# Conversion of W_out through PSUM, and weight sums in halves in other places, in an attention and feed-forward kernel

## The chip, the cores and the metric

The kernel runs on one core of a Trainium2 chip. The metric is the device time of one execution in microseconds (us), measured without a profiler. The profiled execution is a separate one; its span counts from the first to the last instruction.

The core has engines with an instruction stream each: TensorE (PE in the profile, its weight loads are PEld), VectorE (DVE), ScalarE (ACT), GpSimd (POOL), and SyncE (SP), which here only issues transfers (DMA). SBUF is the on-chip memory of 128 partitions, PSUM the smaller one that PE writes its products to; VectorE and ScalarE read and write both.

## The reference

Attention in which a query sees only keys of the same hash bucket, then two matrix products with a gated activation between them. Cut to what matters:

```
def _attn_ref(q, k, v, proj):            # q, k, v: 4 x 8 x 768 x 64, proj: 64 x 6
    q_bits, k_bits = (q @ proj > 0), (k @ proj > 0)
    mask = bucket(q_bits)[..., :, None] == bucket(k_bits)[..., None, :]
    scores = where(mask, q @ k.T / sqrt(64), -1e9)
    return softmax(scores) @ v

def _moe_ref(x, w_in, w_out):            # x: 3072 x 512, w_in: 512 x 2048, w_out: 2048 x 512
    h = x @ w_in
    g = h * (1.0 / (1.0 + np.exp(-1.702 * h)))
    return (g @ w_out).astype(np.float32)
```

The weights w_in and w_out come as numbers of 64 bits; the kernel reads them as pairs of 32-bit words (lo, hi) and makes float32 of them on the chip. This is called conversion below.

## The kernel before

The kernel has three stages. In *attention* PE makes scores and values, ScalarE the exponentials; VectorE converts W_in on the side, one chunk of 128 x 512 numbers at a time. In the *hidden layer* PE makes x @ w_in by one level of Strassen's method (seven products of quarters instead of eight): 24 steps of seven products of 128 x 512, three times 1024 tokens (sb) by eight blocks of 128 rows (mt). Each step stores seven blocks to memory (g_dram): the four activated results and three sums that the next stage needs. In the *output stage* PE makes g @ w_out by two levels of Strassen: 3 x 7 outer products (OUTER), each of seven inner products.

Strassen's method needs sums of the quarters of each factor (`sums_a` for weights, `sums_b` for the data):

```
    def sums_a(eng, a11, a12, a21, a22, s1, s2, s4):
        return [lambda: eng.tensor_tensor(s1, a21, a22, op=Alu.add),
                lambda: eng.tensor_tensor(a21, a11, a21, op=Alu.subtract),     # in place
                lambda: eng.tensor_tensor(s2, s1, a11, op=Alu.subtract),
                lambda: eng.tensor_tensor(s4, a12, s2, op=Alu.subtract)]
```

The conversion of one chunk, seven VectorE instructions and one of ScalarE (the `yield`s are places where other work goes between):

```
    def convert(cv, dst, src, queue=None):
        raw = cv.tile([P, CW, 2], U32, tag="raw", name="raw")
        (queue or loader[0]).dma_start(out=raw, in_=src)
        ...
        lo, hi = raw[:, :, 0], raw[:, :, 1]
        sign, bits, size = ...                                  # three tiles of 128 x 512 in SBUF
        yield
        nc.vector.scalar_tensor_tensor(sign, hi, 0x80000000, masks[0x40000000], op0=Alu.bitwise_and, op1=Alu.bitwise_or)
        nc.vector.scalar_tensor_tensor(bits, hi, 3, masks[0x7FFFFFFF], op0=Alu.logical_shift_left, op1=Alu.bitwise_and)
        yield
        nc.vector.tensor_tensor(bits, bits, sign, op=Alu.bitwise_xor)
        yield
        nc.vector.tensor_tensor(sign, bits, masks[0xFF800000], op=Alu.bitwise_and)
        nc.scalar.activation(size, hi.bitcast(F32), Act.Square)
        yield
        nc.vector.scalar_tensor_tensor(dst, of(lo), 2.0**-52, of(sign.bitcast(F32)), op0=Alu.mult, op1=Alu.mult)
        yield
        nc.vector.tensor_tensor(dst, of(bits.bitcast(F32)), dst, op=Alu.add)
        yield
        nc.vector.scalar_tensor_tensor(dst, of(size), (1.125 * 2.0**-15) ** 2, dst, op0=Alu.is_ge, op1=Alu.mult)
```

`masks[...]` is a column of 128 values spread over 512 elements, so it is a second operand in SBUF. `raw` has one buffer.

One step of the hidden layer:

```
            def hidden(sb, mt, mid=(), end=()):
                ...
                nc.scalar.copy(u, product(1))
                nc.vector.tensor_tensor(v, product(6), u, op=Alu.add)          # evictions: PSUM + SBUF -> SBUF
                nc.vector.tensor_tensor(c21, product(7), v, op=Alu.add)
                p = product(5)
                nc.vector.tensor_tensor(c22, p, c21, op=Alu.add)
                emit(c22, 3)                                                   # activation, store
                nc.vector.tensor_tensor(c12, p, v, op=Alu.add)
                nc.vector.tensor_tensor(u, product(2), u, op=Alu.add)
                emit(u, 0)
                for x in mid:
                    x()
                nc.vector.tensor_tensor(c12, product(3), c12, op=Alu.add)
                emit(c12)
                nc.vector.tensor_tensor(c21, product(4), c21, op=Alu.add)
                emit(c21, 2)
                for f, kept in zip(sums_b(nc.gpsimd, u, c12, c21, c22, v, t2, t4), ((4, v), (1, c12), (5, t2), (6, t4))):
                    f()                                                        # GpSimd's sums of g, stored
                    keep(*kept)
                for x in end:
                    x()
```

What is hung into the steps, and the places of the weights' sums (`rooms`: three sums for each of the seven outer products):

```
            rooms = [xT[:, 3, 0:W2]] + [w_room[:, i * W2 : (i + 1) * W2] for i in range(5)] + [s_room[:, 0:W2]]   # w_room: W_in's tile
            ...
                    if n == 1:
                        ...                                     # w_out_sb; wqs: its quarters and their sums
                        for i in (list(range(1, LATE + 1)) if late else []) + free[:FC]:
                            todo[i] = [lambda: next(steps)] * 2                # one conversion in step i
                        w_steps = sums_a(nc.vector, *wqs)
                        todo[3 * MT - 3], todo[3 * MT - 2] = w_steps[:2], w_steps[2:] + sums_a(nc.gpsimd, *w_quarters(OUTER[0]))
                    if n == 2:
                        ...                                     # two more PSUM banks for products: 6 -> 8
                    if n == 3 * MT - 3:
                        ...
                        fetch(0)
                    if sb == 0 and mt + 1 < MT:
                        for f in in_sums(mt + 1):               # GpSimd: sums of W_in for the next step
                            f()
                    x = sums_b(nc.vector, *quarters_x(sb + 1)) if mt == MT - 1 and sb + 1 < n1 else []
                    hidden(sb, mt, x[:3], x[3:] + todo.pop(n, []) + (g_sums(0) if n == 3 * MT - 1 else []))
            ...
            for n, (sb, o) in enumerate(steps_out):             # output stage
                if n + 1 < len(steps_out):
                    fetch(n + 1)
                if n + 1 < len(OUTER):
                    for f in sums_a(nc.gpsimd, *w_quarters(OUTER[n + 1])):     # inner sums of the next outer product
                        f()
                later_sums = g_sums(n + 1)                      # VectorE: sums of g for the next step
                ...
                ms[o] = product_of_halves(n, None if acc is None else ms[acc], after)
```

In `product_of_halves` the products come in the order 1, 2, 3, 6, 7, 5, 4; only from product 6 on are the sums of g (t2, t1, t4) needed. MT is 8, FC is 16, P is 128.

Of the kernel before, what the change touches and what calls it, by code (L numbers as in the profile page):

```python
# [8 lines left out]
F32 = mybir.dt.float32  # L9
BF16 = mybir.dt.bfloat16  # L10
I32 = mybir.dt.int32
U32 = mybir.dt.uint32
Act = mybir.ActivationFunctionType
Alu = mybir.AluOpType
AX = mybir.AxisListType
PSUM = bass.MemoryType.PSUM
# [3 lines left out]
P = 128  # L20
# [18 lines left out]
def kernel(  # L39
# [17 lines left out]
    nc = tc.nc  # L57
# [8 lines left out]
    KC, FC = DM // P, FF // P  # L66
# [70 lines left out]
    xT = const.tile([P, KC, N], F32, name="xT")  # L137
    w_in_sb = const.tile([P, KC, FF], F32, name="w_in_sb")
    s_in = const.tile([P, 3, KC // 2, FF // 2], F32, name="s_in")
# [9 lines left out]
    CW = 512  # L149


    masks = {}
    for x in (0x40000000, 0x7FFFFFFF, 0xFF800000):
        m = const.tile([P, 1], U32, name=f"mask_{x:x}")
        later.append((m, x))
        masks[x] = m.to_broadcast([P, CW])

    def convert(cv, dst, src, queue=None):

        raw = cv.tile([P, CW, 2], U32, tag="raw", name="raw")  # L160
        (queue or loader[0]).dma_start(out=raw, in_=src)

        def of(x):
            return x if len(dst.shape) == 2 else x.rearrange("p (x r) -> p x r", r=dst.shape[2])

        lo, hi = raw[:, :, 0], raw[:, :, 1]
        sign = cv.tile([P, CW], U32, tag="sign", name="sign")
        bits = cv.tile([P, CW], U32, tag="bits", name="bits")
        size = cv.tile([P, CW], F32, tag="size", name="size")
        yield  # L170

        nc.vector.scalar_tensor_tensor(sign, hi, 0x80000000, masks[0x40000000], op0=Alu.bitwise_and, op1=Alu.bitwise_or)  # L172
        nc.vector.scalar_tensor_tensor(bits, hi, 3, masks[0x7FFFFFFF], op0=Alu.logical_shift_left, op1=Alu.bitwise_and)  # L173
        yield
        nc.vector.tensor_tensor(bits, bits, sign, op=Alu.bitwise_xor)  # L175
        yield

        nc.vector.tensor_tensor(sign, bits, masks[0xFF800000], op=Alu.bitwise_and)  # L178

        nc.scalar.activation(size, hi.bitcast(F32), Act.Square)  # L180
        yield
        nc.vector.scalar_tensor_tensor(dst, of(lo), 2.0**-52, of(sign.bitcast(F32)), op0=Alu.mult, op1=Alu.mult)  # L182
        yield
        nc.vector.tensor_tensor(dst, of(bits.bitcast(F32)), dst, op=Alu.add)  # L184
        yield

        nc.vector.scalar_tensor_tensor(dst, of(size), (1.125 * 2.0**-15) ** 2, dst, op0=Alu.is_ge, op1=Alu.mult)

    wi = w_in.bitcast(U32).rearrange("(kc ki) (f two) -> kc ki f two", ki=P, two=2)
    wo = w_out.bitcast(U32).rearrange("(fc fi) (d two) -> fc fi d two", fi=P, two=2)  # L190
# [3 lines left out]

    LATE = 2

    def sums_a(eng, a11, a12, a21, a22, s1, s2, s4):

        return [lambda: eng.tensor_tensor(s1, a21, a22, op=Alu.add),
                lambda: eng.tensor_tensor(a21, a11, a21, op=Alu.subtract),  # L200
                lambda: eng.tensor_tensor(s2, s1, a11, op=Alu.subtract),
                lambda: eng.tensor_tensor(s4, a12, s2, op=Alu.subtract)]

# [8 lines left out]
    K2, F2 = KC // 2, FF // 2  # L212
# [448 lines left out]
    def feed_forward(tag, late=()):  # L661
# [3 lines left out]
        F4, TH = FC // 4, XT // 2  # L665
        n1 = N // (2 * XT)

        LEFT = dict(zip(range(1, 8), (0, 1, 6, 3, 4, 5, 2)))
        RIGHT = dict(zip(range(1, 8), (0, 2, 3, 6, 4, 5, 1)))
        OUTER = (1, 6, 7, 5, 2, 3, 4)  # L670
        with ExitStack() as fctx:
            stage_ctx = fctx.enter_context(ExitStack())
            stage = stage_ctx.enter_context(tc.tile_pool(name=f"stage{tag}", bufs=2, side="right"))
            late = list(late)
            sets = [fctx.enter_context(tc.tile_pool(name=f"f0{tag}", bufs=6, space=PSUM, side="right"))]
            todo, turn = {}, [-1]
# [46 lines left out]

            wqs = []

            w_room, s_room = (x.rearrange("p k f -> p (k f)") for x in (w_in_sb, s_in[:, 2]))
            W2 = 3 * F4 * P
            rooms = [xT[:, 3, 0:W2]] + [w_room[:, i * W2 : (i + 1) * W2] for i in range(5)] + [s_room[:, 0:W2]]
            wholes = [xT[:, i, 4 * XT : 6 * XT] for i in range(4)] + [t_x[:, i].rearrange("p k t -> p (k t)") for i in range(2)]
            wholes = [x.rearrange("p (q t) -> p q t", q=4) for x in wholes]  # L730

            def w_quarters(o):

                w = wqs[LEFT[o]]
                x = [w[:, i, F4 * j : F4 * (j + 1), :] for i in range(2) for j in range(2)]
                s = rooms[OUTER.index(o)].rearrange("p (i c d) -> p i c d", i=3, c=F4)
                return x + [s[:, i] for i in range(3)]

            steps_out = [(sb, o) for sb in range(n1) for o in OUTER]
            raw_g = [None, s_in[:, 0:2].rearrange("p i k f -> p (i k f)").rearrange("p (c t) -> p c t", t=XT)]  # L740

            def fetch(n):
                sb, o = steps_out[n]
                for h in range(2):
                    cs = slice(h * F4, (h + 1) * F4)
                    loader[0].dma_start(out=raw_g[n % 2][:, cs], in_=g_dram[len(LEFT) * sb + RIGHT[o], :, cs, :])
# [14 lines left out]
            def g_sums(n):  # L761
                return sums_b(nc.vector, *g_quarters(n)) if n < len(steps_out) else [lambda: None] * 4
# [54 lines left out]
                after(3)  # L817
                return m

            def conversions(cv, chunks):  # L820

                gens = [convert(cv, *x) for x in chunks]
                next(gens[0])
                for i, x in enumerate(gens):
                    for y in gens[i + 1 : i + 2]:
                        next(y)
                    for at, _ in enumerate(x):
                        if at == 1:
                            yield
                    yield  # L830

            MT = FC // 2
            for sb in range(n1):
                for mt in range(MT):
                    n = sb * MT + mt
                    if n == 1:
                        wop = fctx.enter_context(tc.tile_pool(name=f"wo{tag}", bufs=1))
                        cv_ctx = fctx.enter_context(ExitStack())
                        cv = cv_ctx.enter_context(tc.tile_pool(name=f"cv{tag}", bufs=1))


                        w_out_sb = wop.tile([P, 4, FC, P], F32, name="w_out_sb")
                        wqs += [w_out_sb[:, 2 * i : 2 * i + 2, MT * k : MT * (k + 1), :] for i in range(2) for k in range(2)]
                        wqs += [xT[:, i, 0 : 4 * XT].rearrange("p (h c d) -> p h c d", h=2, d=P) for i in range(3)]
                        places = [w_out_sb[:, :, fc, :].rearrange("p r x -> p x r") for fc in range(FC)]
                        steps = conversions(cv, late + [(places[fc], wo[fc]) for fc in range(FC)])
                        free = [i for i in range(LATE + 1, 3 * MT) if i % MT != MT - 1]
                        for i in (list(range(1, LATE + 1)) if late else []) + free[:FC]:
                            todo[i] = [lambda: next(steps)] * 2
                        w_steps = sums_a(nc.vector, *wqs)  # L850
                        todo[3 * MT - 3], todo[3 * MT - 2] = w_steps[:2], w_steps[2:] + sums_a(nc.gpsimd, *w_quarters(OUTER[0]))
                    if n == 2:
                        sets.append(fctx.enter_context(tc.tile_pool(name=f"f1{tag}", bufs=2, space=PSUM)))
                        turn[0] = 7
                    if n == 3 * MT - 3:
                        cv_ctx.close()
                        gp = fctx.enter_context(tc.tile_pool(name=f"gp{tag}", bufs=1))
                        raw_g[0] = gp.tile([P, FC // 2, XT], F32, name="raw_g")
                        fetch(0)
                    if sb == 0 and mt + 1 < MT:  # L860
                        for f in in_sums(mt + 1):
                            f()
                    x = sums_b(nc.vector, *quarters_x(sb + 1)) if mt == MT - 1 and sb + 1 < n1 else []
                    hidden(sb, mt, x[:3], x[3:] + todo.pop(n, []) + (g_sums(0) if n == 3 * MT - 1 else []))
                    yield
            stage_ctx.close()
            st2 = fctx.enter_context(tc.tile_pool(name=f"st2{tag}", bufs=1, side="right"))
# [1 line left out]
            ms, pending = {}, []  # L869
            for n, (sb, o) in enumerate(steps_out):  # L870
                final = n + 1 == len(steps_out)
                if n + 1 < len(steps_out):
                    fetch(n + 1)
                if n + 1 < len(OUTER):
                    for f in sums_a(nc.gpsimd, *w_quarters(OUTER[n + 1])):
                        f()
                later_sums = g_sums(n + 1)
                m = wholes[n % len(wholes)]

# [13 lines left out]
                        written(sb, 0, (0,), loader + [nc.scalar])  # L893

                acc = {6: 1, 7: 6, 2: 1, 3: 6, 4: 7}.get(o)
                ms[o] = product_of_halves(n, None if acc is None else ms[acc], after)

                def flat(x):
# [65 lines left out]
```

## Time and profile before

| | before |
|---|---|
| time, median of 3 | 954.63 us (953.36 to 955.95) |
| span of the profiled execution | 951.8 us |
| mean granted PE clock | 0.975 |
| PE, DVE busy | 890.9, 805.4 us |
| ACT, POOL busy | 312.4, 348.5 us |

Busy shares are means over stages with different limits, so the profile is read by stages: in the row of slices each digit is the busy share, in tenths, of one fortieth of the span. In a timeline line stand the start, the duration, the engine, the line of the kernel, the operation with output<-inputs, their shapes, the count, and in brackets the idle time before it and what ended it. In the list of waits stand engine, line, what was waited for, and then the total in us, how often, and the longest. The ends of matmuls in the profile are modelled; their starts are what the text uses.

### The profile page before, as it was taken

To read this page: it belongs to the slowest core of one execution; us is meant where nothing else is said; L and a number is where in the kernel's file an instruction comes from. 1 tells how busy PE (TensorE), PEld (TensorE's weight loads), DVE (VectorE), ACT (ScalarE), POOL (GpSimd) and SP (SyncE) were. 2 spreads that over 40 slices of the span, in tenths; PEclk is the share of its full clock that TensorE was granted. 3 is DMA by queue.
4 is the path that set the end of the run, shared out by engine and by line. 5 is a ranking of instruction groups with operands and counts; after the bars stand their busy time and mean duration, and the time that the engine had idled before them with its cause. 6 is when DMAs were issued, how large, how long until landed. Compare 5 with 4: busy or idle time off the path is not lost.

```text
span 951.8 us, 11992 instructions
## 1 busy us (share of the span) xinstructions
PE 890.9 (94%) x4077; PEld 509.6 (54%) x4077; DVE 805.4 (85%) x1048; ACT 312.4 (33%) x519; POOL 348.5 (37%) x274
## 2 busy tenths in 40 slices
PE   9999999999999999985998859989788999999995
PEld 4444444444444444432443324433577888888884
DVE  4798888888899648999799997999797986887795
ACT  5667666576675422212122122122100000000000
POOL 4233323333224536683453434546995000000000
PEclk9999999999999999998999979999999999999998
DMA  4543454443541024443444434446735566557634
GB/s 96 116 97 78 87 102 90 83 93 77 102 98 46 1 103 159 159 164 134 155 166 154 177 122 171 171 147 228 249 149 177 177 186 248 169 176 211 217 123 91
DMA packets 169477, 132.01 MB, mean 139 GB/s; under 512 B 123936, under 2 KB 138432, under 8 KB 164032
## 3 DMA queue, kind: packets, MB, share of 16 engines
q1 hardware_dynamic: 167712, 129.69, 45.1%
q10 hardware_dynamic: 1696, 1.48, 0.6%
q8 instruction: 34, 0.56, 0.3%
q14 instruction: 35, 0.29, 0.1%
HBM read 79.69 MB, written 50.33 MB: 137 GB/s over the span
## 4 chain that ended last, share of the span: by engine, by line
PE 61%; DVE 27%; issue 6%; POOL 4%; DMA 1%; ACTq 0%; DVEq 0%; SPq 0%; ACT 0%; POOLq 0%
PE product L792 23%; PE ps L420 15%; PE av L444 13%; PE product L690 5%; DVE bits L173 3%; DVE sign L178 3%; DVE bits L175 3%; DVE w_out_sb L182 3%; PE dn L463 3%; DVE w_out_sb L184 2%; DVE xT L796 2%; DVE sign L172 1%; DVE c L704 1%; DVE v L703 1%; DVE c L715 1%
## 5 line engine op out<-in xcount | busy, mean ns | idle before, releaser
L421 ACT ACTIVATE e<-ps 128x768 f32<-128x768 f32 x192 | 151.4, 812 | 19.1 <-PE ps L420 13.1
L420 PE MATMUL ps<-qT,kT 64*128 64x384 f32 x768 | 155.1, 482 | 0.0
L690 PE MATMUL product<-xT,w_in_sb 128*128 128x512 f32 x288 | 138.4, 603 | 10.3 <-DVE v L703 10.3
L444 PE MATMUL av<-e,v 128*64 128x385 f32 x768 | 130.2, 486 | 0.9 <-ACT xT L457 0.9
L428 POOL TENSOR_TENSOR acc<-e 128x768 f32<-128x768 f32 x32 | 49.3, 1542 | 208.6 <-DVE acc L436 139.5
L698 ACT ACTIVATE c<-c 128x512 f32<-128x512 f32 x72 | 45.4, 630 | 238.5 <-issue 151.2
L690 PE MATMUL product<-t_x,s_in 128*128 128x512 f32 x192 | 97.0, 630 | 25.0 <-DVE t_x L209 19.2
L690 PEld LDWEIGHTS product<-xT,w_in_sb 128*128 128x128 f32 x288 | 54.7, 192 | 82.9 <-issue 60.8
L207 POOL TENSOR_TENSOR v<-c,u 128x512 f32<-128x512 f32 x24 | 41.8, 1741 | 156.1 <-ACT c L698 156.1
L444 PEld LDWEIGHTS av<-e,v 128*64 128x64 f32 x768 | 54.9, 136 | 70.6 <-issue 69.0
L420 PEld LDWEIGHTS ps<-qT,kT 64*128 64x128 f32 x768 | 68.2, 188 | 35.5 <-issue 35.5
L690 PEld LDWEIGHTS product<-t_x,s_in 128*128 128x128 f32 x192 | 38.5, 203 | 76.5 <-issue 65.0
L798 ACT COPY u<-product 128x256 f32<-128x256 f32 x21 | 7.8, 371 | 176.1 <-PE product L792 131.8
L420 PE MATMUL ps<-qf,kf 64*128 64x384 bf16 x384 | 63.0, 324 | 0.7 <-ACT e L421 0.5
L429 POOL TENSOR_TENSOR acc<-acc,e 128x768 f32<-128x768 f32 x32 | 56.8, 1773 | 2.5
L792 PE MATMUL product<-raw_g,w_out_sb 128*128 128x256 f32 x192 | 45.3, 387 | 0.0
L690 PE MATMUL product<-t_x,w_in_sb 128*128 128x512 f32 x96 | 45.1, 592 | 0.0
L690 PE MATMUL product<-xT,s_in 128*128 128x512 f32 x96 | 45.1, 592 | 0.0
L420 PEld LDWEIGHTS <-kf 64*128 64x128 bf16 x384 | 18.9, 94 | 42.2 <-issue 20.7
L173 DVE SCALAR_TENSOR_TENSOR bits<-raw,mask_7fffffff 128x512 uint32<-128x512 uint32 x32 | 41.4, 1293 | 0.0
L208 POOL TENSOR_TENSOR c<-c,c 128x512 f32<-128x512 f32 x24 | 40.2, 1675 | 1.9
L792 PEld LDWEIGHTS product<-raw_g,w_out_sb 128*128 128x128 f32 x192 | 37.5, 195 | 5.9 <-DVE c L706 0.2
(199 smaller groups left out, 1628.0 us busy)
## 6 DMA issues: line engine op xcount, KB each, us to landing
raw_g<-g_dram SPq DMA_DIRECT2D x22, 1024.0 KB
s_in<-g_dram SPq DMA_DIRECT2D x20, 1024.0 KB
g_dram<-c SPq DMA_DIRECT2D x72, 256.0 KB
g_dram<-t SPq DMA_DIRECT2D x48, 256.0 KB
raw<-in_moe_w_out_dram SPq DMA_DIRECT2D x16, 512.0 KB
raw<-in_moe_w_in_dram SPq DMA_DIRECT2D x15, 512.0 KB
v<-in_v_dram SPq DMA_DIRECT2D x32, 192.0 KB
g_dram<-u SPq DMA_DIRECT2D x24, 256.0 KB
```

The lines of the kernel that those rows point to most:

```text
L173: nc.vector.scalar_tensor_tensor(bits, hi, 3, masks[0x7FFFFFFF], op0=Alu.logical_shift_left, op1=Alu.bitwise_and)
L175: nc.vector.tensor_tensor(bits, bits, sign, op=Alu.bitwise_xor)
L207: return [lambda: eng.tensor_tensor(t1, b12, b11, op=Alu.subtract), lambda: eng.tensor_tensor(b12, b22, b12, op=Alu.subtract), lambda: eng ...
L208: lambda: eng.tensor_tensor(b12, b22, b12, op=Alu.subtract),
L420: nc.tensor.matmul(ps[:, j, 0:HS], a[hs, keys], m[hs, cols], start=not last, stop=last)
L421: nc.scalar.activation(es[c][:, kt, :, 0:HS], ps[:, :, 0:HS], Act.Exp, scale=1.0 / D**0.5)
L428: nc.gpsimd.tensor_tensor(acc, es[c][:, 0, :, 0:HS], es[c][:, 1, :, 0:HS], op=Alu.add)
L429: nc.gpsimd.tensor_tensor(acc, acc, es[c][:, 2, :, 0:HS], op=Alu.add)
L444: nc.tensor.matmul(av[D * j : D * (j + 1), :], vt[:, t, j, :], es[c][:, t, j, :], start=(t == 0), stop=(t == T - 1))
L690: nc.tensor.matmul(ps, wq[LEFT[i]][:, kc, :], xq[RIGHT[i]][:, kc, :], start=(kc == 0), stop=(kc == K2 - 1))
L698: nc.scalar.activation(c, c, Act.Gelu_apprx_sigmoid)
L792: nc.tensor.matmul(ps, wq[LEFT[i]][:, c, :], gq[RIGHT[i]][:, c, :], start=(c == 0), stop=(c == F4 - 1))
```

## The change

Five things change. (1) The conversion has six VectorE instructions instead of seven: the sign and the top bit of the exponent are taken from hi by one mask, joined with the shifted rest in the same instruction, and the step that put a product into dst now puts it into a tile `part`. (2) In the feed-forward part `part` and `size` lie in PSUM (a pool `cps` of two banks, kept to step 20), and constants take the place of the masks in SBUF. (3) The sums of W_out's quarters are made in two halves (`low`, `high`), each when its half of W_out is converted; the order of conversion follows. (4) The inner sums of the weights get places of their own that come free step by step, and are made in steps 18, 19 and 21 to 23 and in the output stage; the order of the outer products changes from 1, 6, 7, 5, 2, 3, 4 to 1, 2, 6, 7, 5, 3, 4. (5) The sums of g for the first output step are split over steps 22 and 23, and the second fetch moves into step 23. It is for giving VectorE less to do in the hidden layer, with operands that GpSimd doesn't share, and for having the weights' sums ready when the output stage begins.

The core of the diff:

```diff
-    def convert(cv, dst, src, queue=None):
+    def convert(cv, dst, src, queue=None, psum=None):
...
-        sign = cv.tile([P, CW], U32, tag="sign", name="sign")
         bits = cv.tile([P, CW], U32, tag="bits", name="bits")
-        size = cv.tile([P, CW], F32, tag="size", name="size")
+        part = (cv if psum is None else psum).tile([P, CW], U32, tag="part", name="part")
+        size = (cv if psum is None else psum).tile([P, CW], F32, tag="size", name="size")
...
-        nc.vector.scalar_tensor_tensor(sign, hi, 0x80000000, masks[0x40000000], op0=Alu.bitwise_and, op1=Alu.bitwise_or)
-        nc.vector.scalar_tensor_tensor(bits, hi, 3, masks[0x7FFFFFFF], op0=Alu.logical_shift_left, op1=Alu.bitwise_and)
+        if psum is None:
+            nc.vector.scalar_tensor_tensor(part, hi, 3, masks[0x3FFFFFFF], op0=Alu.logical_shift_left, op1=Alu.bitwise_and)
+        else:
+            nc.vector.tensor_scalar(part, hi, 3, 0x3FFFFFFF, op0=Alu.logical_shift_left, op1=Alu.bitwise_and)
         yield
-        nc.vector.tensor_tensor(bits, bits, sign, op=Alu.bitwise_xor)
+        nc.vector.scalar_tensor_tensor(bits, hi, 0xC0000000, part, op0=Alu.bitwise_and, op1=Alu.bitwise_or)
         yield
-        nc.vector.tensor_tensor(sign, bits, masks[0xFF800000], op=Alu.bitwise_and)
+        if psum is None:
+            nc.vector.tensor_tensor(part, bits, masks[0xFF800000], op=Alu.bitwise_and)
+        else:
+            nc.vector.tensor_scalar(part, bits, 0xFF800000, None, op0=Alu.bitwise_and)
         nc.scalar.activation(size, hi.bitcast(F32), Act.Square)
+        part = part.bitcast(F32)
         yield
-        nc.vector.scalar_tensor_tensor(dst, of(lo), 2.0**-52, of(sign.bitcast(F32)), op0=Alu.mult, op1=Alu.mult)
+        nc.vector.scalar_tensor_tensor(part, lo, 2.0**-52, part, op0=Alu.mult, op1=Alu.mult)
         yield
-        nc.vector.tensor_tensor(dst, of(bits.bitcast(F32)), dst, op=Alu.add)
+        nc.vector.tensor_tensor(dst, of(bits.bitcast(F32)), of(part), op=Alu.add)
...
-        OUTER = (1, 6, 7, 5, 2, 3, 4)
+        OUTER = (1, 2, 6, 7, 5, 3, 4)
...
+            s_room = s_in[:, 2].rearrange("p k f -> p (k f)")
+            rooms = [x[:, i * F4 * P : (i + 1) * F4 * P].rearrange("p (c d) -> p c d", d=P)
+                     for x in (xT[:, 3], s_room) for i in range(4)]
+            rooms[4:4] = [w_in_sb[:, :, F2 * i + mt * P : F2 * i + (mt + 1) * P] for mt in range(FC // 2) for i in range(2)]
...
+                        cps = cv_ctx.enter_context(tc.tile_pool(name=f"cps{tag}", bufs=1, space=PSUM))
...
+                        order = [8 * k + 4 * c + i for c in range(2) for k in range(2) for i in range(4)]
+                        chunks = [(w_out_sb[:, :, fc, :].rearrange("p r x -> p x r"), wo[fc]) for fc in order]
+                        steps = conversions(cv, cps, late + chunks)
...
-                        w_steps = sums_a(nc.vector, *wqs)
-                        todo[3 * MT - 3], todo[3 * MT - 2] = w_steps[:2], w_steps[2:] + sums_a(nc.gpsimd, *w_quarters(OUTER[0]))
-                    if n == 2:
+                        low, high = (sums_a(nc.vector, *(x[:, :, F4 * c : F4 * (c + 1), :] for x in wqs)) for c in range(2))
+                        first = 2 * MT + 1
+                        for i, f in enumerate(low):
+                            todo[first + i] = todo[first + i] + [f]
+                        todo[first + 1] = todo[first + 1] + inner_sums(0)[:2]
+                        todo[first + 2] = todo[first + 2] + inner_sums(0)[2:]
+                        todo[first + 4] = high + inner_sums(1)
+                        todo[first + 5] = inner_sums(2)
+                        todo[first + 6] = inner_sums(3)
+                    if n == 3 * MT - 3:
+                        cv_ctx.close()
                         sets.append(fctx.enter_context(tc.tile_pool(name=f"f1{tag}", bufs=2, space=PSUM)))
                         turn[0] = 7
-                    if n == 3 * MT - 3:
-                        cv_ctx.close()
...
-                    hidden(sb, mt, x[:3], x[3:] + todo.pop(n, []) + (g_sums(0) if n == 3 * MT - 1 else []))
+                    t = {3 * MT - 2: g_sums(0)[:2], 3 * MT - 1: g_sums(0)[2:]}.get(n, []) if n > 3 * MT - 3 else []
+                    hidden(sb, mt, x[:3] + ([lambda: fetch(1)] if n == 3 * MT - 1 else []), x[3:] + t + todo.pop(n, []))
...
-                if n + 1 < len(steps_out):
+                if 0 < n and n + 1 < len(steps_out):
                     fetch(n + 1)
-                if n + 1 < len(OUTER):
-                    for f in sums_a(nc.gpsimd, *w_quarters(OUTER[n + 1])):
-                        f()
+                for f in inner_sums(n + 4):
+                    f()
```

`inner_sums(at)` makes the four inner sums of the outer product at this place of OUTER on GpSimd; for place 0 the third result gets a place of its own instead of overwriting a quarter.

## The prediction

> **What bounds the kernel now.** I read the slices of the span first, then the engine shares of single stretches, then the timeline of one step, then what the matrix engine waited for.
>
> ```profile
> PE   9999999999999999985998859989788999999995
> DVE  4798888888899648999799997999797986887795
> POOL 4233323333224536683453434546995000000000
> ```
>
> One digit is 23.8 us. Attention (to 334 us) and the last 210 us have PE at 9: PE sets their time. Between lie slices with PE at 5, 7 or 8 and DVE at 9: there VectorE sets it. The engine shares of three stretches (PE, PEld, DVE, ACT, POOL busy, PE clock, DMA share, GB/s) say the same; the last one is a stretch of the output stage with nothing in PE's way:
>
> ```profile
> 460.00:577.00 117.00, 101.07 (x227) 43.55 (x226) 107.29 (x110) 27.76 (x48) 50.76 (x32) 0.94 0.44 158
> 577.00:690.00 113.00, 102.95 (x259) 50.21 (x258) 102.26 (x99) 26.03 (x45) 67.43 (x40) 0.97 0.54 191
> 729.00:940.00 211.00, 210.80 (x977) 185.62 (x978) 172.84 (x295) 12.66 (x34) 0.00 (x0) 1.00 0.56 182
> ```
>
> The timeline of VectorE and GpSimd through one step of the hidden layer (start, duration, engine, line, operation):
>
> ```profile
> 637.87 0.68 DVE L172 SCALAR_TENSOR_TENSOR sign<-raw,mask 128x512 uint32<-128x512 uint32 x1
> 638.09 1.60 POOL L207 TENSOR_TENSOR v<-c,u 128x512 f32<-128x512 f32 x1 [7.95 <-ACT c L698]
> 638.47 1.77 DVE L173 SCALAR_TENSOR_TENSOR bits<-raw,mask_7fffffff 128x512 uint32<-128x512 uint32 x1
> 640.27 1.64 DVE L175 TENSOR_TENSOR bits<-bits,sign 128x512 uint32<-128x512 uint32 x1
> 641.95 1.64 DVE L178 TENSOR_TENSOR sign<-bits,mask_ff 128x512 uint32<-128x512 uint32 x1
> 643.62 2.00 DVE L182 SCALAR_TENSOR_TENSOR w_out_sb<-raw,sign 128x512 f32<-128x512 uint32 x1
> 645.66 1.05 DVE L184 TENSOR_TENSOR w_out_sb<-bits,w_out_sb 128x512 f32<-128x512 f32 x1
> 646.81 1.03 DVE L187 SCALAR_TENSOR_TENSOR w_out_sb<-size,w_out_sb 128x512 f32<-128x512 f32 x1
> 647.75 0.69 DVE L703 TENSOR_TENSOR v<-product,u 128x512 f32<-128x512 f32 x1
> ```
>
> One conversion fills VectorE from 637.87 to 647.75: 9.88 us. The seven evictions before it took 633.20 to 637.87: 4.67 us. Their sum is the step, 14.55 us. PE needs less: a product in a fully busy stretch starts every 1.717 us (the first step runs from 334.46 to 346.48), so seven need 12.02 us. VectorE is 2.5 us per step too slow.
>
> The same instructions took 0.68 to 0.69 us in attention while GpSimd was idle (216.94 to 219.72 us, one starting every 0.73 us). Here four of them take 1.64 to 2.00 while GpSimd's sums run. The evictions, which read one operand from PSUM, take 0.68 in either case. PE's waits show where else time goes:
>
> ```profile
> PE product L690 <- DVE t_x L209: 19.2, 2, 10.4
> PE product L690 <- DVE v L703: 10.3, 7, 2.3
> PE product L792 <- POOL xT L202: 5.2, 1, 5.2
> PE product L792 <- DVE t2g L209: 3.6, 1, 3.6
> PE product L792 <- DVE t2b L209: 2.6, 1, 2.6
> ```
>
> The first is the change to the next 1024 tokens (twice): VectorE, a whole step late, makes the sums of x only then. The last three are the hand-over to the output stage, where GpSimd makes the weights' inner sums at the last moment.
>
> **The ledger.** PE enters the hidden layer at 334.46, leaves it at 670.90: 336.4 us. Its floor is 24 x 12.02 + 0.9 (attention's last four dn matmuls lie between) = 289.4; 47.0 is lost. The output stage runs from 670.90 to 941.82: 270.9. From 729.20 on, 968 records took 209.18 us, so 56 records (one step) take 12.10 and 21 steps 254.1; 16.8 is lost. The 64 us of loss is all the change can win; attention and the last 10 us stay.
>
> [...] Here the eight records after the 3.62 us wait for t2g took 3.75 us instead of 1.89, so a wait removed brings back nearly 2 us more.
>
> **The change, part by part.**
>
> (a) *Conversion, hidden layer (16 chunks of W_out and 2 late ones of W_in).* Seven VectorE instructions become six, and each of the six has at most one SBUF input: the shift-and-mask and the exponent mask take constants and write PSUM, the others take their second operand (part or size) from PSUM. None should be held up by GpSimd. First one 0.60 (start to start for independent ones, as the evictions), three dependent ones 0.73 each (the spacing in attention), the two that write w_out_sb with a stride 1.15 and 0.95 (L184 and L187 above, start to start, with GpSimd idle): 0.60 + 2.19 + 2.10 = 4.9 us instead of 9.9. VectorE's step becomes 4.67 + 4.9 = 9.6 us, under PE's 12.02. PE becomes the bound. GpSimd's sums shrink as well, from 1.6 to about 1.25 us (L209 at 669.22 took 1.27 beside evictions only): 5 us a step, 8 with the s_in sums of the first steps.
>
> The price is two PSUM banks: products have six until step 20 instead of eight from step 2. Six products are 10.3 us of lead. VectorE's longest pause is 4.9 us plus one half sum of 1.2 to 2.3: room enough.
>
> (b) *Sums of x at the two changes of tokens.* The instructions stay. But with VectorE only one product behind, the first three are done about 1 us after PE ends the step, and PE needs t2 1.7 us after it. I expect the 19.2 us of waiting to vanish and about 1 us each to remain.
>
> (c) *Outer sums of W_out in halves.* Four sums of 2048 elements become eight of 1024. The low four lie one per step in steps 17 to 20 (9.6 + up to 2.3 = 11.9 us, just under PE's step); the high four in step 21, some 9 us beside GpSimd. With 4.67 of evictions this step costs VectorE 13.8 us, which the then eight banks (13.7 us of products) absorb; steps 22 and 23 cost 7 to 9.
>
> (d) *Inner sums.* In the kernel before all seven groups (5 to 8 us of GpSimd each) stand behind step 22; GpSimd runs without a break until 726.5. Now group 0 is made in steps 18 and 19, groups 1 to 3 in steps 21 to 23, groups 4 to 6 in the output stage. The first output step waits for none of them: the 5.2 us go, with their clock penalty. But groups 3 to 6 and the last sums of g are still some 30 us of GpSimd work at the start of the output stage. There VectorE has four sums of 1024 (2.2 each when contended) and five SBUF adds (1.4 each instead of 0.42): 697.43 to 713.3 before, 15.9 us for a 12.1 us step, which led to the 3.6 us wait. I expect this wait and the next to stay, perhaps moved.
>
> (e) *Attention's conversion.* One instruction of 0.69 us less for each of 14 chunks, on an engine that isn't the bound (no wait of PE there is over 1.2 us): 0.
>
> (f) *Fetches.* The second fetch is issued in step 23 instead of behind it: off the path.
>
> Loss left: hidden layer 2 (token changes) + 2 (start and late W_in chunks) = 4 of 47.0; output stage 9 (waits of 3.6 and 2.6 and their slow clock) of 16.8. Saved: 43 + 7.8 = 50.8 us. 954.6 - 50.8 = 904 us.
>
> **Rivals.**
>
> *The bound stays with VectorE.* If the instructions that write PSUM were slow or still held by GpSimd, at 1.65 us for two more of the six, a conversion would take 6.8 us and the step 11.5: still under 12.02. Only all four unstrided ones at 1.65 give 8.7 and a step of 13.4, hence 16 steps with 1.4 us lost and the token changes late again: about 935. Against it speak the evictions, undisturbed at 0.68 beside GpSimd.
>
> *The raw load becomes the wait.* raw has one buffer; its next load stands in SyncE's queue behind the stores of GpSimd's sums (issued at 631.13 for use at 637.87, 6.7 us before need). With steps of 12 us it is issued about 6.5 us after PE ends a step and needed at 12.7: 6.2 us for 512 KB, while the traffic of a step (1.8 MB stored, 0.5 loaded) goes from 158 to 190 GB/s. If it comes 2 us late, VectorE still ends within the step (11.6). If it were to take 10 us, some 2 us a step are lost: about 930.
>
> *The hand-over gets worse.* Work of steps 17 to 23 is now on VectorE and GpSimd together, and eight banks may not cover step 21. That would be 5 to 10 us in place of some I counted as won: 910 to 914.
>
> *Even better.* If no wait remains at the hand-over either, 954.6 - 60 = 895.
>
> **Range and chances.** Centre 904; the better rival gives 895, the hand-over 914, and part of the load or VectorE rival a little over 920. So 895 to 922 for 8 in 10. A gain under 19 us needs the VectorE rival to hold and more: 4 in 100; a loss of over 19 us needs a hold-up of which the trace shows nothing: 1 in 100.
>
> **What would show it.** Right: conversion instructions near 0.68 (the strided two near 1.05) beside GpSimd sums; PE at 9 from 360 to 620 us with product steps of 12.0; the wait for t_x gone from the list; the first output product near 628 us; waits for t2g or t2b of 3 to 8 us in the next 40 us. Wrong: instructions that write PSUM above 1.2 us; SyncE's load of raw ending after VectorE asks for it; PE waits for v in most steps; a step 21 to 23 with PE idle.

## The result, and the profile after

| | before | after |
|---|---|---|
| time, median | 954.38 us (953.36 to 955.95) | 895.36 us (894.04 to 895.53) |
| ratio, 95% interval | | 0.9377 (0.9361 to 0.9393) |
| span of the profiled execution | 951.8 us | 893.7 us |
| hidden layer (floor 289.4) | 336.4 | 289.4 |
| output stage (floor 254.1) | 270.9 | 260.0 |
| DVE, POOL busy | 805.4, 348.5 us | 708.2, 313.0 us |

The stages are read as in the prediction: from PE's first product of the hidden layer (334.18) to its first of the output stage (623.58), and to the modelled end of the output stage's last product (883.57). The slices of the span after the change:

```profile
PE   9999999999999999999999999999989999999995
DVE  4698888888889955777777887888797977897785
POOL 4243233222332363766433444659960000000000
```

The slices with PE at 5 to 8 in the hidden layer are gone, and there DVE stands mostly at 7 or 8 where it stood at 9. One slice with PE at 8 is left in the output stage, the thirtieth (648 to 670 us). The engine shares of the stretches (PE, PEld, DVE, ACT, POOL busy, PE clock, DMA share, GB/s):

```profile
334.20:460.00 125.80, 125.80 (x296) 55.39 (x296) 90.22 (x126) 37.34 (x62) 68.15 (x64) 1.00 0.49 175
460.00:577.00 117.00, 117.00 (x274) 51.87 (x273) 93.39 (x127) 33.99 (x57) 51.54 (x40) 1.00 0.54 192
577.00:623.60 46.60, 46.60 (x110) 20.54 (x109) 40.89 (x46) 12.65 (x22) 35.84 (x25) 1.00 0.60 211
623.60:671.00 47.40, 43.55 (x193) 37.43 (x192) 40.54 (x49) 3.24 (x8) 37.32 (x22) 0.96 0.60 209
```

In the first three, the whole hidden layer, PE is busy for every microsecond at a granted clock of 1.00. In the fourth, the start of the output stage, 3.9 us are missing. The timeline of VectorE and GpSimd through one conversion:

```profile
479.29 1.27 POOL L216 TENSOR_TENSOR v<-c,u 128x512 f32<-128x512 f32 x1 [6.80 <-ACT c L707]
480.19 0.68 DVE L177 TENSOR_SCALAR part<-raw 128x512 uint32<-128x512 uint32 x1
...
480.90 0.69 DVE L179 SCALAR_TENSOR_TENSOR bits<-raw,part 128x512 uint32<-128x512 uint32 x1
481.62 0.69 DVE L185 TENSOR_SCALAR part<-bits 128x512 uint32<-128x512 uint32 x1
482.35 0.69 DVE L190 SCALAR_TENSOR_TENSOR part<-raw,part 128x512 f32<-128x512 uint32 x1
483.08 1.05 DVE L192 TENSOR_TENSOR w_out_sb<-bits,part 128x512 f32<-128x512 f32 x1
484.24 1.04 DVE L195 SCALAR_TENSOR_TENSOR w_out_sb<-size,w_out_sb 128x512 f32<-128x512 f32 x1
485.20 0.68 DVE L712 TENSOR_TENSOR v<-product,u 128x512 f32<-128x512 f32 x1
```

The six instructions and what lies between take 485.20 - 480.19 = 5.01 us where seven took 9.88, although GpSimd's sums run beside them; and those take 1.27 instead of 1.6. Each of the six has at most one SBUF input. The five that lie wholly beside the sums (479.29 to 484.51) keep 0.68 to 0.69 and 1.05, also the two that have a single tile as input, read from SBUF, and write PSUM (L177 and L185). Of PE's waits in the feed-forward part the list keeps one of any size:

```profile
PE product L812 <- DVE t2g L218: 3.5, 1, 3.5
```

It lies in the third output step. (t2g and t2b are the two tiles that take turns in holding the sum t2 of g.) The timeline shows what delays it:

```profile
650.32 2.29 DVE L216 TENSOR_TENSOR t<-raw_g 128x1024 f32<-128x1024 f32 x1
...
655.08 1.95 DVE L218 TENSOR_TENSOR t2g<-raw_g,t 128x1024 f32<-128x1024 f32 x1
656.03 2.13 POOL L209 TENSOR_TENSOR w_out_sb<-w_out_sb 128x512 f32<-128x512 f32 x1
...
657.18 3.33 PE L812 MATMUL product<-t2g,w_in_sb 128*128 128x256 f32 x8 [3.47 <-DVE t2g L218]
```

The same sum of 1024 elements takes 1.22 us while GpSimd is idle (at 679.88). Here GpSimd makes the inner sums of later steps without a break, VectorE's sums take 1.6 to 2.3, and PE waits 3.47 us for t2g. The eight records after it (the matmuls of one product) take 3.33 us instead of 1.89, at a granted clock of 0.57.

### The profile page after: what moved, and what is told of

It reads as the page before. It is cut to its first block, busy times and chain, and to the rows that moved or that the text cites. A ratio compares the mean times of both kernels' runs of the same rounds, so it can differ in the third digit from the quotient of the medians.

```text
span 893.7 us, 11965 instructions
## 1 busy us (share of the span) xinstructions
PE 875.1 (98%) x4077; PEld 504.9 (56%) x4077; DVE 708.2 (79%) x1020; ACT 313.6 (35%) x519; POOL 313.0 (35%) x273
## 4 chain that ended last, share of the span: by engine, by line
PE 89%; DVE 3%; POOL 3%; issue 1%; DMA 1%; ACTq 0%; SPq 0%; ACT 0%; POOLq 0%; DVEq 0%
PE product L699 30%; PE product L812 25%; PE ps L429 16%; PE av L453 14%; PE dn L472 3%; PE hash L405 1%; DVE xT L816 1%; POOL c L217 1%; DMA q<-in_q_dram 1%; POOL t L218 1%; POOL t L219 1%; POOL v L216 1%; PE tp L363 0%; POOL w_in_sb L208 0%; ACTq L417 0%
## 5 line engine op out<-in xcount | busy, mean ns | idle before, releaser
L699 PE MATMUL product<-xT,w_in_sb 128*128 128x512 f32 x288 | 135.4, 592 | 0.0
L699 PE MATMUL product<-t_x,s_in 128*128 128x512 f32 x192 | 90.2, 592 | 0.0
L216 POOL TENSOR_TENSOR v<-c,u 128x512 f32<-128x512 f32 x24 | 34.2, 1425 | 129.3 <-ACT c L707 129.3
L699 PEld LDWEIGHTS product<-t_x,s_in 128*128 128x128 f32 x192 | 36.5, 190 | 45.9 <-issue 43.8
L479 DVE STREAM_TRANSPOSE rt<-dn 128x384 f32<-128x384 f32 x32 | 18.6, 580 | 25.7 <-PE dn L472 25.6
L465 ACT COPY vs<-av 128x1 f32<-128x1 f32 x32 | 5.1, 159 | 95.1 <-PE av L453 95.0
L812 PE MATMUL product<-raw_g,xT 128*128 128x256 f32 x152 | 35.5, 382 | 0.0
L490 DVE TENSOR_TENSOR xT<-xT,rt 128x384 f32<-128x384 f32 x32 | 32.6, 1019 | 1.7
```

Source lines behind the costliest of these rows:

```text
L216: return [lambda: eng.tensor_tensor(t1, b12, b11, op=Alu.subtract), lambda: eng.tensor_tensor(b12, b22, b12, op=Alu.subtract), lambda: eng ...
L479: nc.vector.transpose(rt, dn)
L490: nc.vector.tensor_tensor(x_of(n, c), x_of(n, c), rt.rearrange("p (t s) -> p t s", t=GT), op=Alu.mult)
L699: nc.tensor.matmul(ps, wq[LEFT[i]][:, kc, :], xq[RIGHT[i]][:, kc, :], start=(kc == 0), stop=(kc == K2 - 1))
L812: nc.tensor.matmul(ps, wq[LEFT[i]][:, c, :], gq[RIGHT[i]][:, c, :], start=(c == 0), stop=(c == F4 - 1))
```

## The experiments

The theory has two parts. First, the conversion was slow because VectorE and GpSimd held each other up in SBUF; with PSUM operands this ends, VectorE's step falls below PE's 12.02 us, and that is the hidden layer's whole gain. Second, the sums' new places bring the gain at the hand-over, and what is lost there still is the inner sums of late steps made too early. The rivals: the gain is that of one instruction fewer; it is that of the sums' places; the wait that remains comes from a late start of VectorE's sums and not from GpSimd.

**Six steps, but in SBUF** (the changed kernel; the six-instruction conversion keeps `part`, `size` and the masks in SBUF):

```diff
-                gens = [convert(cv, *x, psum=psum) for x in chunks]
+                gens = [convert(cv, *x) for x in chunks]
```

> The changed kernel with part, size and the masks of the six-step conversion in SBUF again; nothing else differs. Theory (the shared operand path with GpSimd is the cause): four of the six instructions have two SBUF inputs and take 1.6 to 2.0 us beside GpSimd's sums, a conversion takes 8.5 to 9 us, VectorE's step 13.2 to 13.7 us, over PE's 12.02, and the changes of tokens cost again: 920 to 938 us. Rival (six instructions instead of seven is the cause): within 3 us of the changed kernel, 893 to 899.

Measured: 938.94 us, 0.9842 (0.9823 to 0.9861) of the time before; hidden layer 323.5, output stage 268.7. Lines of its timeline, one conversion:

```profile
510.66 1.65 DVE L179 SCALAR_TENSOR_TENSOR bits<-raw,part 128x512 uint32<-128x512 uint32 x1
511.83 1.60 POOL L217 TENSOR_TENSOR c<-c,c 128x512 f32<-128x512 f32 x1
512.34 1.64 DVE L183 TENSOR_TENSOR part<-bits,mask_ff 128x512 uint32<-128x512 uint32 x1
```

Both engines are slow again: 1.64 where the changed kernel has 0.69, and 1.60 where it has 1.28. All six instructions have two SBUF inputs here, where the expectation counts four; the four that start while GpSimd's sums run (510.17 to 516.77) are slow, the first and the last take 0.68 and 1.04. A conversion lasts 8.80 us (509.94 to 518.74), VectorE's step 13.47. Six instructions and the new places of the sums are together worth 15 us this way; the other 44 hang on where the operands lie. The scratch tiles in PSUM and the constants in place of the masks go together in all these runs, so their shares are not known apart. The time is 1 us above the expected range.

**The conversion alone** (the kernel before with the PSUM conversion; the two extra banks for products open in step 21; all sums as before):

```diff
-                gens = [convert(cv, *x) for x in chunks]
+                gens = [convert(cv, *x, psum=psum) for x in chunks]
...
-                    if n == 2:
-                        sets.append(fctx.enter_context(tc.tile_pool(name=f"f1{tag}", bufs=2, space=PSUM)))
-                        turn[0] = 7
                     if n == 3 * MT - 3:
                         cv_ctx.close()
+                        sets.append(fctx.enter_context(tc.tile_pool(name=f"f1{tag}", bufs=2, space=PSUM)))
+                        turn[0] = 7
```

> The kernel before with the conversion through PSUM alone; the weights' sums stay whole and where they were. Theory: PE runs the hidden layer at its floor (289 to 292 us, t_x waits gone), and the hand-over loses what it lost before, 17 us or a little more, as the sums of W_out still lie at its end: 905 to 913 us. Rival (the new places of the sums carry the gain): over 930.

Measured: 904.64 us, 0.9479 (0.9461 to 0.9498), 0.4 us below the range. The first products of the hidden layer and of the output stage:

```profile
334.89 1.02 PE L698 MATMUL product<-xT,w_in_sb 128*128 128x512 f32 x2
...
624.28 3.62 PE L800 MATMUL product<-raw_g,w_out_sb 128*128 128x256 f32 x16
```

The hidden layer takes 289.4, as with the whole change, so the conversion alone brings all 47 us of it. The output stage takes 268.3, with PE waits of 5.5 for t2g, 3.3 for t2b and 1.2 for GpSimd's w_in_sb.

**The sums' places alone** (the changed kernel with the seven-instruction conversion in SBUF, its whole text taken from the kernel before):

```diff
-    def convert(cv, dst, src, queue=None, psum=None):      # six instructions
+    def convert(cv, dst, src, queue=None):                 # seven instructions, as before
...
-                gens = [convert(cv, *x, psum=psum) for x in chunks]
+                gens = [convert(cv, *x) for x in chunks]
```

> The changed kernel with the old seven-step conversion in SBUF; the sums in halves and in their new places stay. Theory: VectorE's step is 14.5 us again, 16 in the four steps with a half sum, the hidden layer loses 47 us or more, and only the hand-over's 10 us are won: 940 to 952 us. Rival (the sums carry the gain): 895 to 915.

Measured: 960.51 us, 1.007 (1.0051 to 1.009): 0.7% slower than before, and outside the range. The hidden layer takes 342.8 instead of 336.4, the output stage 270.3. The timeline of VectorE and GpSimd in step 18 shows why:

```profile
616.05 1.96 POOL L200 TENSOR_TENSOR xT<-w_out_sb 128x512 f32<-128x512 f32 x1
617.03 1.87 DVE L184 TENSOR_TENSOR w_out_sb<-bits,w_out_sb 128x512 f32<-128x512 f32 x1
...
619.00 1.91 DVE L187 SCALAR_TENSOR_TENSOR w_out_sb<-size,w_out_sb 128x512 f32<-128x512 f32 x1
620.83 1.21 DVE L201 TENSOR_TENSOR w_out_sb<-w_out_sb 128x1024 f32<-128x1024 f32 x1
```

VectorE is the bound in this step. The half sum adds its 1.21 us, and GpSimd's inner sums, new here, stretch L184 and L187 from 1.05 to 1.9. From the half sum of step 17 (603.44) to that of step 18 is 17.4 us, where a step took 14.55. This run also keeps the changed kernel's six banks for products until step 20, but at the start of step 17, counted from the start of the layer, PE is 0.4 us ahead of the kernel before; the loss comes after it, and how much of it the fewer banks make there isn't shown. At the output stage next to nothing is won. So parts (3) to (5) of the change, which were not tried apart, are together worth 268.3 - 260.0 = 8.3 us of the output stage with the fast conversion, and cost 6 us without it: the parts of this change don't add.

**GpSimd's sums left out** (the kernel before; four of the seven blocks that a step stores are these sums, three are activated results; here v and c12 go out without their sum, and c21, c22 stand in for t2, t4, so the outputs are not the reference's):

```diff
-                for f, kept in zip(sums_b(nc.gpsimd, u, c12, c21, c22, v, t2, t4), ((4, v), (1, c12), (5, t2), (6, t4))):
-                    f()
+                for kept in ((4, v), (1, c12), (5, c21), (6, c22)):
                     keep(*kept)
```

> The kernel before, with GpSimd's four sums of g in each step of the hidden layer left out (other tiles are stored in their place, so the output is not the reference's). VectorE's instructions are the same seven in SBUF. Theory: without GpSimd reading beside them they take 0.68 to 1.15 us, the conversion about 6.0 instead of 9.9 us, the step 10.7, under PE's 12.02; the hidden layer comes near its floor: 898 to 912 us. Rival (the seven instructions with strided and SBUF operands are slow by themselves): the conversion stays above 8.5 us and the time above 935.

Measured: 898.57 us, 0.942 (0.9402 to 0.9439); hidden layer 289.9. The old seven instructions, all in SBUF, with GpSimd idle (its timeline from 503 to 511.5 has no instruction of it):

```profile
504.90 0.68 DVE L173 SCALAR_TENSOR_TENSOR bits<-raw,mask_7fffffff 128x512 uint32<-128x512 uint32 x1
505.62 0.69 DVE L175 TENSOR_TENSOR bits<-bits,sign 128x512 uint32<-128x512 uint32 x1
506.35 0.69 DVE L178 TENSOR_TENSOR sign<-bits,mask_ff 128x512 uint32<-128x512 uint32 x1
```

L173 took 1.77 beside GpSimd, L175 and L178 1.64. A conversion takes 5.99 us (504.30 to 510.29). Nothing of the conversion was edited, and the hidden layer is at its floor: the sharing was the cost, and neither the count of instructions nor SBUF as such.

The output stage is shorter here too, 261.4 instead of 270.9, with no wait for t2b, though all sums of the weights are where they were. GpSimd ends its inner sums 39.9 us after the start of the stage (at 663.81); with the conversion alone it is 52.8 us and the stage takes 268.3, in the changed kernel 38.2 us and 260.0. So what counts at the hand-over may be how much work GpSimd still has there, and the new places are one way to have less; these runs don't separate the two.

**One instruction more, and five more** (the changed kernel; the conversion's first instruction issued twice, and six times):

```diff
-            nc.vector.tensor_scalar(part, hi, 3, 0x3FFFFFFF, op0=Alu.logical_shift_left, op1=Alu.bitwise_and)
+            for _ in range(2):       # five more: range(6)
+                nc.vector.tensor_scalar(part, hi, 3, 0x3FFFFFFF, op0=Alu.logical_shift_left, op1=Alu.bitwise_and)
```

> The changed kernel with the first conversion instruction (raw to part in PSUM) issued twice in the feed-forward part: seven VectorE instructions again, all with at most one SBUF input. Theory: VectorE's step is 4.67 + 5.01 + 0.72 = 10.4 us, under PE's 12.02, so nothing changes: 894 to 898 us. Rival (the count of instructions is what the time follows): 18 conversions x 0.72 = 13 us more, 906 to 910.

Measured with one more: 896.91 us, 0.9389 (0.9373 to 0.9404); hidden layer 289.5. Seven instructions through PSUM do as well as six: the count wasn't the gain, and VectorE has slack.

> The same with this instruction issued six times: 5 x 0.72 = 3.6 us more per conversion. VectorE's step is 13.3 us, 1.3 over PE's 12.02, and over 14.5 in the four steps with a half sum. Theory (VectorE bounds again once its step passes PE's): 18 x 1.3 and 4 x 1.5 us, less what the two steps without a conversion give back (2 x 2.3) and PE's lead: 912 to 926 us. Rival (PSUM operands free VectorE from the bound altogether): under 900.

Measured with five more: 936.12 us, 0.9807 (0.979 to 0.9823), above the range; output stage 266.8. The six issues take 4.34 us together:

```profile
411.73 4.34 DVE L178 TENSOR_SCALAR part<-raw 128x512 uint32<-128x512 uint32 x6
```

VectorE's step is 13.33 us (407.06 to 420.39), over PE's 12.02, and the hidden layer 322.9. PE's waits in it:

```profile
PE product L700 <- DVE v L713: 10.5, 11, 2.2
PE product L700 <- DVE t_x L219: 8.8, 2, 4.4
...
PE product L700 <- DVE w_out_sb L196: 2.2, 1, 2.2
```

The 33.5 us over the floor are 21.5 of waits; the other 12 are not in the list. The granted clock of the execution is 0.980 where the changed kernel has 0.994, by estimate 13 us of its span of 933.4, some of them in the output stage, and the timeline has products after such waits at a lower rate (four records in 3.10 us after 2.17 us of idling, for 1.88). My range took the excess over 12.02 for the steps with a conversion and no token changes, no late hand-over and no slow clock. The kernel with six steps in SBUF has nearly the same step, 13.47, by wholly other means, and the same time to 3 us: it is the length of VectorE's step against PE's that sets the time, wherever it comes from.

**Late inner sums left out** (the changed kernel without the inner sums of outer products 5 to 7; their tiles hold whatever lay there but for a column of zeros, so the output is not the reference's):

```diff
-                for f in inner_sums(n + 4):
-                    f()
+                if n == 0:
+                    for at in (4, 5, 6):
+                        for r in rooms[3 * at + 1 : 3 * at + 4]:
+                            nc.gpsimd.memset(r[:, :, 0:1], 0.0)
```

> The changed kernel with the inner sums of the last three outer products (places 4 to 6, GpSimd's work in the first output steps) left out, so the output is not the reference's. Theory (what is left of the hand-over's loss is VectorE's sums held up by GpSimd's): the wait of 3.5 us for t2g and its slow clock go: 889 to 892 us. Rival (it is the late place of t1b, for which VectorE waits 2.3 us at the start of the stage): the wait stays at 2 to 4 us, 893 to 896.

Measured: 890.15 us, 0.9319 (0.9303 to 0.9334); output stage 254.6, 0.5 above its floor; no wait for t2g:

```profile
650.98 1.22 DVE L218 TENSOR_TENSOR t2g<-raw_g,t 128x1024 f32<-128x1024 f32 x1
```

VectorE's four sums for the third output step take 1.22 or 1.23 us each, while its idling of 2.3 us before t1b (in the changed kernel too; the profile names no releaser) is still there. So the 5 us hang on GpSimd's sums. The late t1b costs at most the 0.6 us that the second step is over its 12.1, 0.3 of them waiting.

**Inner sums paced** (the changed kernel, nothing left out: group 4 of the inner sums leaves step 23, and each later group is made one output step later, held back by a GpSimd copy of one column of the previous step's result):

```diff
-                        todo[first + 6] = inner_sums(3)
...
+            pace = st2.tile([P, 1], F32, name="pace")
...
-                for f in inner_sums(n + 4):
+                if n and inner_sums(n + 3):
+                    nc.gpsimd.tensor_copy(pace, ms[steps_out[n - 1][1]][:, 2, 0:1])
+                for f in inner_sums(n + 3):
                     f()
```

> The changed kernel with the inner sums paced: group k is made in output step k-3, and a small copy on GpSimd of a column that the step before wrote holds it back to that step; so one group stands beside one step instead of three and a half groups in three. The work is the same. Theory: VectorE loses about 4 us a step to one group and has 2.2 us of its own and PE's lead to cover it; the wait shrinks or goes: 889 to 893 us. Rival (only the total of contention counts): 894 to 897.

Measured: 890.67 us (889.81 to 891.38), 0.9323 (0.9307 to 0.9338); output stage 254.6. From the timeline of the third output step:

```profile
652.76 1.22 DVE L218 TENSOR_TENSOR t2g<-raw_g,t 128x1024 f32<-128x1024 f32 x1
652.91 1.11 POOL L905 COPY pace<-xT 128x1 f32<-128x1 f32 x1 [4.41 <-DVE xT L816]
...
654.57 1.89 PE L812 MATMUL product<-t2g,w_in_sb 128*128 128x256 f32 x8
```

GpSimd idles 4.41 us while VectorE makes three of its four sums; t2g is early, and the products that needed it start without a gap. The same work as in the changed kernel, in the same place in memory but later, takes 4.7 us less by the medians. It is the fastest of the measured kernels that leave nothing out.

## What held of the prediction, and which step of it failed

*The mechanism* (a) held: "VectorE's step becomes 4.67 + 4.9 = 9.6 us, under PE's 12.02. PE becomes the bound." The conversion measured 5.01 instead of 4.9, with each instruction at the predicted 0.68 to 0.69 or 1.05. The ground for it was the evictions, which read one operand from PSUM and kept 0.68 beside GpSimd; that the two instructions with a single SBUF tile as input (L177 and L185) would keep their time too was an estimate, and they took 0.68 and 0.69. GpSimd's sums shrank to the predicted 1.27. That the sharing was the cause is shown from both sides: PSUM operands alone, and GpSimd's sums left out, each bring the hidden layer to 289.4 and 289.9.

*The time* was 8.6 us shorter than the 904 us. The step that failed is the sum of what stays lost: "Loss left: hidden layer 2 (token changes) + 2 (start and late W_in chunks) = 4 of 47.0; output stage 9 (waits of 3.6 and 2.6 and their slow clock) of 16.8." It measured 0 and 5.9: PE has no wait in the hidden layer, and of the two waits that it expected to stay at the hand-over only the one for t2g did. Of the slow clock that the sum gives both waits, the kernel before shows only that after the first: eight records in 3.75 us at a granted clock of 0.50 after 3.62 us of waiting (at 711.33), but in 1.97 at 1.00 after 2.55 (at 729.20), instead of 1.89. Of the 8.6 us, 4.0 are the hidden layer's, 3.1 the output stage's and 0.3 an earlier end of attention; the remaining 1.2 is that the spans differ by 58.1 us and the medians by some 59.

- Token changes (b): the working there was better than the sum. It had the first three sums done about 1 us after PE's step and t2 needed at 1.7 us. At the first change PE begins the new tokens at 527.44, the third sum ends at 528.43, and PE takes up t_x at 529.16: 1.0 and 1.7. By these numbers no wait was due, and yet 1 us each was put into the sum, as was 2 for start and late chunks, with no wait behind it. A wait that the prediction doesn't list, 5.6 us for s_in (GpSimd's sums of W_in, three times in the kernel before), is gone too.
- Outer sums in halves (c): the low half sums took 1.2 to 1.95, the high four 8.0 together in step 21 (600.35 to 608.35); PE has no gap there. Right.
- Inner sums (d): "I expect this wait and the next to stay, perhaps moved" was half right. The wait for t2g stayed (3.47 and 1.4 of slow clock). That for t2b, in the fourth output step, is gone; 0.4 of idling stands before the t2b product of the second step. In the kernel with the conversion alone it is 3.3, so parts (3) to (5) removed it; which of them was not tried apart. The prediction also read the lines of VectorE's work there too high: the five SBUF adds took 5.9 us together, 1.2 each and not 1.4, and the four sums 8.0, so 2.0 each and not 2.2; the 15.9 us of the whole stands.
- Attention (e) and fetches (f): within 0.3 us, and no wait for a fetch.

Of the rivals, the load of raw never became the wait: in one step it is issued at 484.95 and first used at 492.20, 7.3 us later, and in no step does VectorE wait for it. "Even better" named 895 us and nearly this time came, but not for its reason: a wait of 3.5 us does remain at the hand-over. The paced version is a whole kernel without it, and lies below 895, at 890.67, because the hidden layer has no loss left either.

## What to carry to other kernels

When VectorE and GpSimd work side by side and both take longer than alone (here 1.64 instead of 0.69 us, and 1.60 instead of 1.27), look for VectorE instructions with two SBUF operands, and put one of them into PSUM if banks can be spared, or a constant in its place and the result into PSUM (the six then took 0.68 to 0.69 and 1.05): here a conversion through PSUM was worth 49 of 59 us, and one instruction more in it cost 1.5, only 0.1 of them in the hidden layer. Shifting work to earlier steps paid here only where those steps had slack on the engine that bounds them: the same shift won 8 us after the bound was lifted, and lost 6 before. When a sum of remaining waits is made, put in only waits for which the timings give a cause, and ask of work that is ready too early what it slows meanwhile.

## What was not expected of the hardware

The instructions that write w_out_sb with a stride take 1.05 us, also with GpSimd idle, against 0.69 for the others of the same size. L182 shows it alone: 0.69 us when it writes a chunk of W_in without a stride (at 219.72 in the kernel before), 1.05 into w_out_sb (at 507.07 with GpSimd's sums left out). The stride costs 0.36 there, and with an operand in PSUM it is the same 1.05 (L192 in the changed kernel). Copying one column of one element per partition on GpSimd (`pace`) took 1.11 us beside a VectorE sum that stayed at 1.22. And the slow clock isn't tied to one length of wait: in the kernel before, two waits of 2.27 us were followed by four records in 1.98 us (at 633.94, granted clock 1.00) and in 3.20 us (at 648.50, 0.60).
